# Moving a kernel's output transfers to another queue, its later states to a DMA transpose, more buffers for one small tile, and two smaller changes at its start

## The chip, the cores and the metric

One core of one Trainium2 chip. The metric is the device time of one execution in microseconds (us), lower is better; several executions are taken and their median is quoted. Beside it stands the **span**, the length of the one profiled execution from its first to its last instruction, which is about 2 us shorter than that execution's time. Executions of one kernel spread by up to some 1.5% here; one that is more than 1.5% above the fastest of its kernel is called slow, and only fast ones are compared. The experiments ran on several chips, and each took the kernel before along on its own chip, which is what the ratios are made of.

## The reference

Eight batches of attention between 512 tokens and 32 states in 8 heads of 64, then a feed-forward block with the maximum of three products, over all 8 × 544 rows.

```python
# x: (8, 8, 512, 64), state: (8, 8, 32, 64)
a  = softmax(scale * x @ state^T);   xread = a @ state
a2 = softmax(scale * state @ x^T);   sread = a2 @ x
y  = concat([xread, sread], axis=2)            # -> rows (batch, 512+32), 512 columns
h  = max(y @ w1, y @ w2, y @ w3)               # w: 512 x 768
out = h @ w_out                                # 768 x 512, float32
```

## The kernel before

A batch is prepared while the one before it goes through the feed-forward block. For a batch, x is loaded and cast by GpSimd's DMA queue (`load_x`), transposed by a DMA on SyncE's queue (`xT`), multiplied with the states (`scores`, which need xT), normalised by GpSimd (`a`), and a is transposed by DMA (`aT`). The second softmax gives `sr`, which a small DMA transpose puts into `ats`. `G` holds the states times the weights, so that `maxout` needs only aT and G.

```python
    def x_transpose_dma(b):
        new(xT, b, [128, H, 2, 128], "xT")
        nc.sync.dma_start_transpose(out=xT[b].rearrange("p h j t -> p (h j) t"), in_=x_sb[b][:, 0:XW])
    # ... cut ...
    def states_rest():
        st = data.tile([128, 16, 2, D], BF16, name="st")
        for c in range(2):
            nc.gpsimd.tensor_copy(out=st[:, :, c, :], in_=st_f)
        # ... cut: 16 TensorE transposes, copies by VectorE and ScalarE into bdr ...
    # ... cut ... end of sread(b):
        sr = work.tile([128, 2, D], BF16, tag="sr", name="sr")          # two buffers
        nc.vector.tensor_mul(out=sr, in0=p[:, :, 0, :], in1=rd.to_broadcast((128, 2, D)))
        late.append(lambda: nc.sync.dma_start_transpose(
            out=ats[:, b].rearrange("p s n -> p (s n)"), in_=sr.rearrange("p g d -> p (g d)")))
    # ... cut ... end of ffn_out(b, j): two transfers of 512 KB for a batch, at j = 1 and j = 3
        j0 = j if b == B - 1 and j >= 2 else j - 1
        if j == 1 or j == 3 or j0 == j:
            nc.sync.dma_start(
                out=out[b * SP:b * SP + S, :].rearrange("(p j) f -> p j f", j=J)[:, j0:j + 1, :],
                in_=o[:, j0:j + 1, :])
    # ... cut ... the loop: six slots for a batch, n = b + 1
            slots[0].append(lambda: scores(n, 0, 2))
            slots[0].append(lambda: softmax(n, 0, 2, nc.gpsimd.tensor_mul))
            slots[1].append(lambda: g_cols(n, (0, 1)))
            slots[2].append(lambda: a_transpose_dma(n))
            slots[3].append(lambda: sread(n))
            # ... cut ...
                slots[3].append(lambda: x_transpose_dma(n + 1))
            slots[4].append(late_transposes)
                slots[1].append(lambda: load_x(n + 2))
        for m in (1, 2, 4, 5):           # ffn_out of the batch before: j = 0, 1, 2, 3
            if pending:
                slots[m].append(lambda t=pending.pop(0): ffn_out(*t))
```

Slot 2 thus issues aT and then the first output of the batch before (j = 1, its half of 512 KB); slot 3 issues xT of the next batch but one.

The softmax here doesn't subtract the row's maximum and nothing guards it: scores larger than these inputs give would overflow.

Of the kernel before, what the change touches and what calls it, by code (L numbers as in the profile page):

```python
# [15 lines left out]
def kernel(  # L16
# [39 lines left out]
    E = 2  # L56
# [30 lines left out]
    def load_w(c):  # L87
        m0, m1 = chunks[c]
        for i, w in enumerate((moe_w1, moe_w2, moe_w3)):
            nc.gpsimd.dma_start(  # L90
                out=w_sb[c][:, :, i, :],
                in_=w.rearrange("(kk p) f -> p kk f", p=128)[:, :, m0 * 128:m1 * 128])

    def w_cols(m):
        c = [m0 <= m < m1 for m0, m1 in chunks].index(True)
        f = (m - chunks[c][0]) * 128
        return w_sb[c], slice(f, f + 128)

    load_w(0)
    bde = data.tile([128, E, H, 2, Ns], BF16, name="bde")  # L100
    nc.vector.memset(bde, 0.0)
# [4 lines left out]
    load_w(1)  # L106
    load_x(1)
    load_w(2)
    load_w(3)
    load_x(2)  # L110
    nc.gpsimd.dma_start(out=wout_sb, in_=moe_w_out.rearrange("(kk p) f -> p kk f", p=128))
# [6 lines left out]
    def keep_busy(n):  # L118
        p = pp.tile([128, 1024], F32, tag="two", name="idle")
        for _ in range(n):  # L120
            nc.tensor.matmul(p[:, 0:512], zero[:, 0:128], zero, start=True, stop=True)
# [4 lines left out]

    def states_early():
        st = data.tile([128, 2 * E, 2, D], BF16, name="ste")
        nc.vector.tensor_copy(out=st, in_=st_early_f.unsqueeze(2).to_broadcast((128, 2 * E, 2, D)))
        p = pp.tile([128, 2 * E, 128], BF16, tag="pw", bufs=4, name="pte")  # L130
        for t in range(2 * E):
            nc.tensor.transpose(p[:, t, :], st[:, t].rearrange("p c d -> p (c d)"), ident)
        for c, copy in enumerate((nc.vector.tensor_copy, nc.scalar.copy)):
            r = slice(64 * c, 64 * c + 64)
            copy(out=bde[r, :, :, c, :].rearrange("p b h n -> p (b h) n"),
                 in_=p[r].rearrange("p t (h n) -> p (t h) n", n=Ns))

    def states_rest():

        st = data.tile([128, 16, 2, D], BF16, name="st")  # L140
        for c in range(2):
            nc.gpsimd.tensor_copy(out=st[:, :, c, :], in_=st_f)  # L142
        for k in range(2):
            p = pp.tile([128, 8, 128], BF16, tag="pw", bufs=4, name="pt")
            for t in range(8):
                nc.tensor.transpose(p[:, t, :], st[:, 8 * k + t].rearrange("p c d -> p (c d)"), ident)
            for c, copy in enumerate((nc.vector.tensor_copy, nc.scalar.copy)):
                r = slice(64 * c, 64 * c + 64)
                dst = bdr[r, :, :, c, :].rearrange("p b h (q t) -> p (b h) q t", t=16)
                copy(out=dst[:, :, :, 8 * k:8 * k + 8],  # L150
                     in_=p[r, :, 16 * E:16 * B].rearrange("p t (k q) -> p k q t", q=2))


    xT, e, a, aT, G, ht, osb = {}, {}, {}, {}, {}, {}, {}
# [4 lines left out]
    def x_transpose(b, g, copy):  # L159

        if g == 0:
            new(xT, b, [128, H, 2, 128], "xT")
        p = pp.tile([128, HS, 2, 128], BF16, tag="pw", bufs=4, name="pxt")
        for s in range(HS):
            for jj in range(2):
                nc.tensor.transpose(  # L166
                    p[:, s, jj, :],
                    xv[b][:, 2 * s + g, 2 * jj:2 * jj + 2, :].rearrange("p j d -> p (j d)"), ident)
        copy(out=xT[b].rearrange("p (s g) j t -> p g s j t", g=2)[:, g], in_=p)
# [24 lines left out]
    def softmax(b, g0, g1, mul):  # L194
        n = g1 - g0
        if g0 == 0:
            new(a, b, [128, J, 2, HS, Ns], "a")
        den = work.tile([128, J, n, HS], F32, tag=f"den{n}", name="den")
        nc.vector.reduce_sum(out=den, in_=e[b][:, :, g0:g1], axis=AX.X)  # L199
        rden = work.tile([128, J, n, HS], F32, tag=f"rden{n}", name="rden")  # L200
        nc.vector.reciprocal(out=rden, in_=den)  # L201
        mul(  # L202
            out=a[b][:, :, g0:g1].rearrange("p j g s n -> p j (g s) n"),
            in0=e[b][:, :, g0:g1].rearrange("p j g s n -> p j (g s) n"),
            in1=rden.rearrange("p j g s -> p j (g s)").unsqueeze(3).to_broadcast((128, J, n * HS, Ns)))
# [17 lines left out]
    def sread(b):  # L223

        p = pp.tile([128, 2, 2, D], F32, tag="pw", bufs=4, name="psr")
        for j in range(J):
            for g in range(2):
                for s in range(HS):
                    xj = xv[b][:, 2 * s + g, j, :]
                    both = bass.AP(xj.tensor, xj.offset,  # L230
                                   (xj.ap[0], (XW - ((2 * s + g) * J + j) * D, 2), (1, D)))
                    nc.tensor.matmul(  # L232
                        p[32 * s:32 * s + 32, g], e[b][:, j, g, s, :], both,
                        start=(j == 0 and g == 0), stop=(j == J - 1), skip_group_check=True,
                        tile_position=(0, 32 * s))
        rd = work.tile([128, 2, 1], F32, tag="rd", name="rd")
        nc.vector.reciprocal(out=rd, in_=p[:, :, 1, 0:1])
        sr = work.tile([128, 2, D], BF16, tag="sr", name="sr")
        nc.vector.tensor_mul(out=sr, in0=p[:, :, 0, :], in1=rd.to_broadcast((128, 2, D)))  # L239
        late.append(lambda: nc.sync.dma_start_transpose(  # L240
            out=ats[:, b].rearrange("p s n -> p (s n)"), in_=sr.rearrange("p g d -> p (g d)")))


    def g_cols(b, ms):
        for m in ms:
            if m == 0:
                new(G, b, [128, 2, NM * 384], "G")
            w, f = w_cols(m)
            p = pp.tile([128, 2, 512], F32, tag="two", name="pg")
            for s in range(HS):  # L250
                for g in range(2):
                    nc.tensor.matmul(  # L252
                        p[32 * s:32 * s + 32, g, 0:384].rearrange("p (i f) -> p i f", i=3),
                        bd(b, 2 * s + g)[64 * g:64 * g + 64, g, :], w[64 * g:64 * g + 64, s, :, f],
                        start=True, stop=True, tile_position=(64 * g, 32 * s))
            nc.scalar.copy(out=G[b][:, :, m * 384:(m + 1) * 384], in_=p[:, :, 0:384])  # L256


    def maxout(b, m, n, lhs, rhs, nk):
# [14 lines left out]
    def x_maxout(b, m):  # L274
        maxout(b, m, 512,
               lambda i, k: G[b][:, k, m * 384 + i * 128:m * 384 + i * 128 + 128],
               lambda k: aT[b][:, :, k, :], 2)
# [6 lines left out]
    def ffn_out(b, j, split=False):  # L284
        if j == 0:
            osb[b] = work.tile([128, J, d_model], F32, tag="osb", name="osb")
        p = pp.tile([128, d_model], F32, tag="pw", bufs=4, name="po")
        for m in range(NM):
            nc.tensor.matmul(p, ht[b][:, m, j * 128:(j + 1) * 128], wout_sb[:, m, :],  # L289
                             start=(m == 0), stop=(m == NM - 1))  # L290
        o = osb[b]
        if split:
            nc.scalar.copy(out=o[:, j, 0:256], in_=p[:, 0:256])
            nc.vector.tensor_copy(out=o[:, j, 256:512], in_=p[:, 256:512])
        else:
            nc.scalar.copy(out=o[:, j, :], in_=p)  # L296
        if b == "s":
            for k in range(4 * j, 4 * j + 4):
                r0 = k * SP + S
                (nc.sync if k % 4 < 2 else nc.gpsimd).dma_start(  # L300
                    out=out[r0:r0 + Ns, :], in_=o[32 * (k % 4):32 * (k % 4) + 32, j, :])
            return
        j0 = j if b == B - 1 and j >= 2 else j - 1
        if j == 1 or j == 3 or j0 == j:
            nc.sync.dma_start(
                out=out[b * SP:b * SP + S, :].rearrange("(p j) f -> p j f", j=J)[:, j0:j + 1, :],
                in_=o[:, j0:j + 1, :])

# [3 lines left out]
            late.pop(0)()  # L312

    dve, act = nc.vector.tensor_copy, nc.scalar.copy
    keep_busy(5)
    states_early()
    dve(out=xv[0].rearrange("p (s g) j d -> p g s (j d)", g=2)[:, 0], in_=x0_f[0])
    act(out=xv[0].rearrange("p (s g) j d -> p g s (j d)", g=2)[:, 1], in_=x0_f[1])
    x_transpose(0, 0, dve)
    x_transpose(0, 1, dve)  # L320
    for g in range(2):
# [3 lines left out]
    a_transpose(0, 0, act)  # L325
    a_transpose(0, 1, dve)
    x_maxout(0, 0)
    g_cols(0, (1, 2))
    sread(0)
    x_transpose(1, 0, dve)  # L330
    x_transpose(1, 1, dve)
    x_maxout(0, 1)
    scores(1, 0, 2)
    softmax(1, 0, 2, nc.gpsimd.tensor_mul)
    x_maxout(0, 2)
    g_cols(0, (3,))
    g_cols(1, (0, 1))
    x_maxout(0, 3)
    sread(1)
    g_cols(0, (4, 5))  # L340
    states_rest()
    x_transpose_dma(2)
    x_maxout(0, 4)
    g_cols(1, (2, 3))
    a_transpose(1, 0, act)
    a_transpose(1, 1, dve)
    x_maxout(0, 5)
    g_cols(1, (4, 5))


    pending = [(0, j) for j in range(J)]
# [63 lines left out]
```

## Time and profile before

| | before |
|---|---|
| time | 182.09 us, median of 3 (180.52 to 182.64) |
| span | 179.5 us, mean granted TensorE clock 0.968 |
| scores matmuls of batches 2 to 7 start at | 36.47, 61.29, 79.86, 98.38, 115.73, 131.86 |
| periods between them | 24.8, 18.6, 18.5, 17.35, 16.1 |

The kernel has one spine: the scores matmuls of each batch. Nothing of a batch can go on before them, so their distance is the batch's period, and the time is *start of the first of the steady ones + five periods + a tail*. Here 36.47 + 95.39 + 47.64 = 179.5. (The prediction reads the last two starts as 115.89 and 132.02; the timeline's rows have 115.73 and 131.86, and nothing hangs on that.)

The two views to hold on to are the shares of the chain that ended last, and the list of DMA issues (transfer, queue that issued it, count, KB of each, median us from issue to landing). Before:

```profile
PE 55%; DMA 16%; DVE 13%; ACT 5%; SPq 4%; issue 3%; POOL 2%; DVEq 0%; ACTq 0%; POOLq 0%
...
out_dram<-osb SPq DMA_DIRECT2D x15, 512.0 KB, 3.0
...
xT<-x SPq DMA_TRANSPOSE x6, 9.5
```

The chain runs mostly through TensorE. The median output lands 3.0 us after it was issued and the median xT after 9.5 us, from the same queue. A median hides something here: the four outputs that are issued just ahead of an xT, with x's load still running, take 6.5 to 9.4 us.

### The profile page before, as it was taken

Reading aid. Unit: us, or ns where it says so; the run is one execution under the profiler, and the core shown is the slowest. Engines: PE = TensorE matmul, PEld = TensorE weight load, DVE = VectorE, ACT = ScalarE, POOL = GpSimd, SP = SyncE. Lnnn points to the kernel's source line nnn. Section 1 sums busy time; section 2 is a strip of 40 time slices with the busy share of each in tenths; the row PEclk is TensorE's granted clock in tenths of the full one; section 3 lists DMA queues with packets and bytes.
Section 4 is the critical chain, followed back from the end, with each engine's and each line's share of the span. In section 5 each row is a group of like instructions: output and inputs, shape, how many; then the busy total and the mean of one; then the engine's idle time right before and its main releaser. Section 6 shows DMA issues by size and latency. Waiting matters only on the chain.

```text
span 179.5 us, 3488 instructions
## 1 busy us (share of the span) xinstructions
PE 151.5 (84%) x1390; PEld 70.0 (39%) x1405; DVE 96.3 (54%) x167; ACT 96.4 (54%) x153; POOL 34.5 (19%) x39
## 2 busy tenths in 40 slices
PE   5467975899806999949995999999999999999991
PEld 1242633343301434423432344434344447566440
DVE  5384885675205386437653636486557638555200
ACT  3342675894501774828373646783785582344340
POOL 8774252006000050003200230040004000000040
PEclk9999999999975999999999699999999999999998
DMA  4999999902991209990795269617631502020354
GB/s 138 300 194 190 195 201 200 138 5 40 198 171 23 109 14 121 201 198 17 96 216 108 117 82 226 167 64 168 135 121 23 160 4 119 0 117 0 121 197 155
DMA packets 39008, 22.64 MB, mean 126 GB/s; under 512 B 24464, under 2 KB 36496, under 8 KB 38992
## 3 DMA queue, kind: packets, MB, share of 16 engines
q1 hardware_dynamic: 23936, 15.21, 36.7%
q0 software_dynamic: 14528, 7.08, 30.8%
q8 instruction: 11, 0.18, 0.4%
q10 hardware_dynamic: 528, 0.13, 0.3%
q14 instruction: 5, 0.04, 0.1%
HBM read 15.34 MB, written 8.91 MB: 135 GB/s over the span
## 4 chain that ended last, share of the span: by engine, by line
PE 55%; DMA 16%; DVE 13%; ACT 5%; SPq 4%; issue 3%; POOL 2%; DVEq 0%; ACTq 0%; POOLq 0%
PE pw L266 27%; PE po L289 19%; DMA xT<-x 12%; DVE den L199 4%; SPq L173 4%; ACT e L192 3%; PE pg L252 3%; DVE ht L272 3%; DMA stef<-in_state_dram 3%; DVE t L271 2%; PE ps L187 2%; PE pxt L166 2%; DMA ats<-sr 1%; PE psr L232 1%; POOL st L142 1%
## 5 line engine op out<-in xcount | busy, mean ns | idle before, releaser
L266 PE MATMUL pw<-aT,G 128*128 128x512 bf16 x288 | 74.9, 392 | 8.9 <-DVE sr L239 6.7
L271 DVE TENSOR_TENSOR t<-t,pw 128x512 bf16<-128x512 bf16 (+1 forms) x54 | 35.0, 649 | 41.7 <-ACT t L270 38.8
L289 PE MATMUL po<-wout,ht 128*128 128x512 bf16 x189 | 48.5, 383 | 1.0 <-issue 0.2
L266 PEld LDWEIGHTS <-G 128*128 128x128 bf16 x288 | 27.3, 100 | 42.6 <-issue 7.9
L270 ACT CAST t<-pw 128x512 bf16<-128x512 f32 (+1 forms) x54 | 30.6, 566 | 23.8 <-PE pw L266 22.3
L256 ACT CAST G<-pg 128x768 bf16<-128x768 f32 x48 | 36.0, 802 | 12.2 <-PE pg L252 11.9
L272 DVE TENSOR_TENSOR ht<-t,pw 128x512 bf16<-128x512 bf16 (+1 forms) x54 | 35.5, 657 | 5.6
L202 POOL TENSOR_TENSOR a<-e,rden 128x1024 bf16<-128x1024 bf16 x7 | 13.3, 1905 | 99.6 <-DVE rden L201 53.9
L296 ACT COPY osb<-po 128x512 f32<-128x512 f32 x33 | 19.3, 585 | 23.2 <-PE po L289 22.8
L289 PEld LDWEIGHTS <-ht 128*128 128x128 bf16 x204 | 18.6, 98 | 25.7 <-issue 7.0
L199 DVE TENSOR_REDUCE den<-e 128x32 f32<-128x1024 bf16 (+1 forms) x9 | 9.9, 1099 | 7.0 <-ACT e L192 7.0
L192 ACT ACTIVATE e<-ps 128x1024 bf16<-128x1024 f32 x7 | 7.2, 1023 | 9.3 <-PE ps L187 9.3
L252 PE MATMUL pg<-w,bdr 64*32 64x384 bf16 x288 | 10.0, 347 | 0.0
L90 POOL DMA_DIRECT2D w<-in_moe_w_dram x12 | 9.4, 799 | 2.4 <-DMA w<-in_moe_w_dram 2.3
L300 POOL DMA_DIRECT2D out_dram<-osb x4 | 2.1, 523 | 35.3 <-ACT osb L296 35.1
L266 PE MATMUL pw<-ats,w 128*128 128x256 bf16 x72 | 8.8, 273 | 0.0
L187 PEld LDWEIGHTS <-xT 128*128 128x128 bf16 x128 | 5.1, 102 | 7.2 <-DMA xT<-x 5.5
L266 PEld LDWEIGHTS <-w 128*128 128x128 bf16 x72 | 7.0, 98 | 2.1
L187 PE MATMUL ps<-bdr,xT 128*128 128x64 bf16 x96 | 3.8, 193 | 4.5 <-DMA xT<-x 4.5
L239 DVE TENSOR_TENSOR sr<-psr,rd 128x128 bf16<-128x128 f32 x8 | 2.3, 291 | 9.0 <-DMA ats<-sr 8.8
L79 POOL DMA_DIRECT2D x<-in_x_dram x7 | 6.4, 918 | 0.6 <-DMA w<-in_moe_w_dram 0.6
L252 PEld LDWEIGHTS <-bdr 64*32 64x32 bf16 x288 | 2.5, 90 | 8.4 <-issue 8.4
(46 smaller groups left out, 56.5 us busy)
## 6 DMA issues: line engine op xcount, KB each, us to landing
out_dram<-osb SPq DMA_DIRECT2D x15, 512.0 KB, 3.0
x<-in_x_dram POOLq DMA_DIRECT2D x7, 512.0 KB, 10.4
w<-in_moe_w_dram POOLq DMA_DIRECT2D x6, 256.0 KB, 9.4
x0f<-in_x_dram SPq DMA_DIRECT2D x2, 512.0 KB, 5.1
w<-in_moe_w_dram POOLq DMA_DIRECT2D x6, 128.0 KB, 8.3
wout<-in_moe_w_out_dram POOLq DMA_DIRECT2D x1, 768.0 KB, 13.1
stf<-in_state_dram SPq DMA_DIRECT2D x1, 512.0 KB, 6.6
out_dram<-osb SPq DMA_DIRECT2D x2, 256.0 KB, 2.2
```

The source lines that it names most:

```text
L187: nc.tensor.matmul(p[:, 2 * jj:2 * jj + 2, g - g0, s, :], xT[b][:, h, jj, :], bd(b, h).rearrange("p c n -> p (c n)"), start=(g == g0 and s ...
L192: nc.scalar.activation(out=e[b][:, :, g0:g1], in_=p, func=AF.Exp, scale=scale)
L199: nc.vector.reduce_sum(out=den, in_=e[b][:, :, g0:g1], axis=AX.X)
L202: mul(out=a[b][:, :, g0:g1].rearrange("p j g s n -> p j (g s) n"), in0=e[b][:, :, g0:g1].rearrange("p j g s n -> p j (g s) n"), in1=rden.r ...
L252: nc.tensor.matmul(p[32 * s:32 * s + 32, g, 0:384].rearrange("p (i f) -> p i f", i=3), bd(b, 2 * s + g)[64 * g:64 * g + 64, g, :], w[64 * ...
L256: nc.scalar.copy(out=G[b][:, :, m * 384:(m + 1) * 384], in_=p[:, :, 0:384])
L266: nc.tensor.matmul(p[:, 0:n], lhs(i, k), rhs(k), start=(k == 0), stop=(k == nk - 1))
L270: nc.scalar.copy(out=t0[:, 0:n], in_=pw[0][:, 0:n])
L271: nc.vector.tensor_max(t1[:, 0:n], t0[:, 0:n], pw[1][:, 0:n])
L272: nc.vector.tensor_max(ht[b][:, m, :], t1[:, 0:n], pw[2][:, 0:n])
L289: nc.tensor.matmul(p, ht[b][:, m, j * 128:(j + 1) * 128], wout_sb[:, m, :], start=(m == 0), stop=(m == NM - 1))
L296: nc.scalar.copy(out=o[:, j, :], in_=p)
```

## The change

Its intent: keep output transfers from standing between the transposes on SyncE's queue; take work off TensorE, VectorE and ScalarE at the start; have TensorE at full clock when data arrives; remove a wait for the two `sr` buffers. The diff, with the parts that only follow from it cut, as is the move of one early block of G ahead of another:

```diff
+    st = data.tile([128, 16, 2, D], BF16, name="st")
+    stT = data.tile([128, 16, 128], BF16, name="stT")
+    def states_rest_cast():            # called after load_w(2), ahead of load_w(3), load_x(2)
+        for c in range(2):
+            nc.gpsimd.tensor_copy(out=st[:, :, c, :], in_=st_f)
+        nc.sync.dma_start_transpose(out=stT, in_=st.rearrange("p t c d -> p (t c d)"))
 ...
-    def states_rest():                 # casts, 16 TensorE transposes, copies by VectorE, ScalarE
+    def states_rest_place():
         for c in range(2):
+            r = slice(64 * c, 64 * c + 64)
+            nc.gpsimd.tensor_copy(
+                out=bdr[r, :, :, c, :].rearrange("p b h (q t) -> p (b h) q t", t=16),
+                in_=stT[r, :, 16 * E:16 * B].rearrange("p t (k q) -> p k q t", q=2))
 ...
-        sr = work.tile([128, 2, D], BF16, tag="sr", name="sr")
+        sr = work.tile([128, 2, D], BF16, tag="sr", bufs=B, name="sr")
 ...
-            nc.sync.dma_start(
+            (nc.sync if b == B - 1 else nc.gpsimd).dma_start(
                 out=out[b * SP:b * SP + S, :]. ... [:, j0:j + 1, :], in_=o[:, j0:j + 1, :])
 ...
-    keep_busy(5)
+    keep_busy(12)
 ...                                    # early copies: ste by ScalarE, x of batch 0 by VectorE
-    g_cols(0, (1, 2))
+    g_cols(0, (1, 2), (act, dve))      # and three more of batch 1
```

## The prediction

> **What bounds the kernel now.** I read the page first (busy shares, the forty slices), then the chain of work that ended last in order of time, then TensorE's own waits, then the SyncE queue's timeline. The page's slices:
>
> ```profile
> PE   5467975899806999949995999999999999999991
> PEclk9999999999975999999999699999999999999998
> DMA  4999999902991209990795269617631502020354
> ```
>
> A slice is 179.5/40 = 4.49 us. TensorE is nearly full from slice 12 on, so the second two thirds are bound by matmuls. It is not full in slices 0 to 11, and slice 11 is empty; where it was empty the granted clock falls (slices 11, 12, 22). DMA is full from slice 1 to slice 7 (4.5 to 36 us) and again in bursts. TensorE's waits, from 40 to 170 us, are few and large:
>
> ```profile
> PE pw L266 <- DVE sr L239: 6.7, 1, 6.7
> PE ps L187 <- DMA xT<-x: 4.5, 2, 2.3
> PE pw L266 <- DVE ht L272: 1.0, 5, 0.2
> ```
>
> The chain shows how the 6.7 us comes about, and the shape of one of the two 2.3 us waits:
>
> ```profile
> 46.15 6.30 SPq L173
> 52.50 2.32 DMA ats<-sr
> 54.92 0.30 DVE sr L239
> 55.27 2.74 PE pw L266 x6
> ...
> 66.13 0.59 PE pw L266 x2
> 66.72 1.31 PE po L289 x6
> 68.06 0.59 ACT osb L296
> 68.67 0.43 SPq L305
> 69.19 10.63 DMA xT<-x
> 79.86 0.65 PE ps L187 x16
> ```
>
> First group: there are only two sr buffers. VectorE cannot write batch 2's sr until batch 0's sr has been transposed out, and that transpose stands in the SyncE queue behind the 512 KB transpose xT (its issue alone took 7.87 us). VectorE stops, PSUM is not emptied, TensorE stops, and the next six matmuls take 2.74 us where six otherwise take 1.3: it came back at half clock. Second group: xT of the next batch is issued only after an output transfer, which itself waited for ScalarE's osb. The transpose lands 10.63 us later and the scores matmuls wait for it. The SyncE queue's timeline:
>
> ```profile
> 66.83 1.26 SPq L218 DMA_TRANSPOSE aT<-a  x1
> 68.67 0.43 SPq L305 DMA_DIRECT2D out_dram<-osb  x1
> 69.19 7.27 SPq L173 DMA_TRANSPOSE xT<-x  x1
> ```
>
> So a batch's period is the distance between scores matmuls. In the timeline these start at 36.47, 61.29, 79.86, 98.38, 115.89 and 132.02: periods of 24.8, 18.6, 18.5, 17.5, 16.1. The last has no x load beside it and no wait; I take **16.1 us as the TensorE-bound period**.
>
> **What the Trainium skill says.** (1) "DMA: Bandwidth & Descriptors", section "Issuing engines are not separate DMA queues": transfers issued by any engine end on the same 16 DMA engines, and a second issuer saves only issue time. The trace agrees as to rate: from 10 to 33 us the bytes per second stay near 200 GB/s, whether the GpSimd queue runs alone or xT runs beside it. (2) The same page, "Queues, rings and completion order", says that an engine takes turns between queues, packet by packet. The trace hardly shows turns: xT of batch 2, issued at 26.57, moved no packet until about 30.6, while 200 to 350 packets per us went on the GpSimd queue. The measurement decides: a transpose issued into a backlog waits for much of it. (3) "TensorE: Matmul & The Clock Gate", "Part 1: The HAM clock gate": half clock by default, full clock after about 3.4 us of sustained work, measured in a free-running window. The trace agrees: the five warm-up matmuls start 0.43 us apart, end at 3.5 us and did not suffice; 128x512 matmuls still come 0.42 us apart at 16 us and 0.215 us apart after 19.5 us. (4) "SBUF — State Buffer" warns that some VectorE operations lock GpSimd out of writing its descriptors. The trace of before can't show this for outputs; its x loads in the loop issue in 0.94 us beside a busy VectorE, so I charge nothing for it.
>
> **The change part by part.**
> *Eight sr buffers.* The write-after-read wait goes, with it the 6.7 us and the cold restart (2.74 - 1.3 = 1.4 us, and 0.3 us on the next sixteen): 8.4 us on the path. The period 24.8 becomes at best 16.1, else whatever xT allows.
>
> *Outputs on the GpSimd queue.* Eleven or so 512 KB outputs leave the SyncE queue; aT is then followed directly by xT. At the chain above xT could issue at 66.83 + 1.26 = 68.1 in place of 69.19: 1.1 us earlier. It also no longer stands behind the output in its own ring. Packets per us show that xT's bulk ran only after that output had landed (issued 87.25, landed after 9.4, i.e. 96.6; 1,707 of xT's 2,048 packets moved from 96 to 98). What remains ahead of xT is x's load (active 88 to 93.5). Against that the output now stands in the loads' queue, behind which transposes seem to wait. GpSimd pays an issue of 0.5 to 0.9 us per output (rows of 523 and 918 ns) and is 19% busy; in its order every output precedes only work that comes later anyway. Estimate: xT 0.5 to 2 us earlier, periods 18.6 and 18.5 become about 17.2, 17.5 becomes 17.2.
>
> *Later states by DMA transpose.* Removed: sixteen transposes on TensorE (1.07 us), 1.81 us of VectorE, 1.66 us of ScalarE, and the wait for GpSimd's casts: in the chain from 26.26 to 31.6, of which some 4 us are on the path. Added: one transpose of 128x2048 bf16, the size of xT, in the time when DMA is full. Alone xT takes 3.4 us of issue and lands after 5.2. The DMA was busy until 35.57, when xT of batch 2 landed (26.57 + 9.0), only 0.7 us before the scores matmul that reads it. With 2.5 to 3.4 us more to move, it lands at 38 to 39. Then GpSimd places the states: 2 copies of 1536 elements per partition, at the 1.03 us per 1024 of its casts some 1.5 us each, 3.1 us in all; if the states' transpose waits for the load backlog (to 31 us) it lands at 34 to 35.5 and the placing ends at 37.5 to 39. Either way scores of batch 2 start at about **38.8**, not 36.47: 2.3 us **lost**.
>
> *Warm-up of 12 and shared copies.* 12 x 0.43 = 5.2 us from 1.19: TensorE is busy to 6.3 and should then run at full clock. The path from 6.02 to 17.73 holds about 6 us of TensorE at half clock, so 3 us less, and ste and x move off each other's engine for a little more. But batch 1's x lands at 17.15 (the GpSimd queue waits for it until then) and its transposes ran at 18.67: at most 1.5 us of it survive there, and TensorE, which I expect at batch 2's scores by about 32, then waits some 6 us for xT. Value at the end: nothing.
>
> **Sum.** Scores of batch 2 at 38.8; four periods of 17.2 with x loads (68.8), one of 16.1: the last scores matmul at 123.7 where it was 132.0. After it nothing changes but the outputs' queue: 179.5 - 132.0 = 47.5, so a span of 171.2. The profiled run's time exceeded its span by 1.9 (181.42 against 179.5) and the median is 0.7 above that run: 171.2 + 2.6 = 173.8. I state 174.3, as the wait at 32 to 38 may bring the half clock back.
>
> **Rivals.** (a) *Transposes starve behind the outputs too.* The GpSimd queue then carries x and two outputs per batch, and xT lands no earlier than before: periods stay at 18.5. For it: the silent 4 us after 26.57, and that all bytes still cross the same engines. Against: xT's bulk followed the output's landing, in its own ring. Result: 38.8 + 4 x 18.5 + 16.1 + 47.5 = 176.4, as a time 179. (b) *The start hides or costs more.* If GpSimd's strided placing takes 3 us a copy in place of 1.5, or the casts, now ahead of four loads, delay batch 2's x by their 2 us, the loop begins at 41 to 42: 2 to 3 us worse, 176 to 177. Conversely, if the DMA had slack for the states' transpose, it begins at 35: 170. (c) *TensorE-bound loop.* If xT is out of the way entirely, periods are 16.1: 4.4 us better, about 170. For it: only 2.3 us separate before from this.
>
> **Range and chances.** A and b together give just over 181, c with an early start 166. Neither end is likely; 8 in 10 from 169.5 to 179.5. Faster by 2% means under 178.4: only with rival a and some of b is it missed, 0.83. Within 2% 0.15; slower needs a new stall that I do not see, 0.02.
>
> **What would show each step.** Right: no wait for sr in TensorE's list, and periods of 16 to 17.5 between scores matmuls; xT issued directly behind aT; TensorE idle before batch 2's scores, released by xT or by the placed states (bdr), with scores at 37.5 to 40; transposes at 7 us at full clock (0.5 us for eight), yet batch 1's transposes not before 17.2. Wrong: periods of 18.5 with xT as releaser (rival a); scores of batch 2 before 36.5 (the DMA had slack); a wait of softmax on GpSimd behind an output; half clock before slice 4. The prediction fails as a whole if the start loses more than 6 us or the clock falls in several slices of the loop.

## The result, and the profile after

| | before | after |
|---|---|---|
| time, same chip | 182.37 us (180.52 to 183.33, 4 runs) | 198.81 us (197.65 to 201.02, 4 runs, the last slow) |
| ratio of fast runs | | 1.0917, 95% interval 1.0795 to 1.1039 |
| span, granted clock | 179.5 us, 0.968 | 196.9 us, 0.904 |
| scores of batch 2 start at | 36.47 | 40.01 |
| periods of batches 2→3 … 6→7 | 24.8, 18.6, 18.5, 17.35, 16.1 | 21.7, 22.9, 23.4, 23.5, 17.7 |
| xT landing after its issue, batches 3, 4, 5, 6 | 10.0, 10.6, 10.6, 8.0 | 14.5, 15.6, 16.1, 16.1 |

A ratio here is the mean time of one kernel's fast runs over that of the other's fast runs of the same rounds, so it is not quite the ratio of the medians quoted.

The kernel is 9% slower where 4% faster was expected. The span grew by 17.4 us: 3.5 up to the scores of batch 2, 13.8 in the five periods (109.2 against 95.4), 0.1 in the tail. The slices (tenths of busy time and of the clock in 40 equal parts of the span) after:

```profile
PE   7619959489964999289970999529999999999991
PEclk9975996969996699969996699957999999999999
DMA  5999999904999099913999069990952232011065
```

TensorE now has a hole in each of batches 3 to 6 (4, 2, 0 and 2 in slices 12, 16, 21 and 26), and at or behind each hole the clock falls to 6 or 5. Before, there were two such places. TensorE's waits from 40 to 170 us (line, what it waited for, us in all, times, longest) give one cause:

```profile
PE ps L189 <- DMA xT<-x: 24.2, 5, 6.1
```

The wait for sr, 6.7 us before, is gone. In its place the scores wait 24.2 us for xT, 4.5 before; 3.3 of the 24.2 are the wait before batch 2, the rest are the four holes. Chain shares and DMA issues, in the view shown of before:

```profile
DMA 50%; issue 21%; PE 14%; POOL 8%; SPq 2%; ACT 2%; DVE 2%; POOLq 0%; ACTq 0%; DVEq 0%
...
out_dram<-osb POOLq DMA_DIRECT2D x14, 512.0 KB, 6.2
...
xT<-x SPq DMA_TRANSPOSE x6, 15.0
```

Half of the chain is now DMA. One batch of it, in order of time (start, us, what):

```profile
113.99 1.25 SPq L220
...
115.28 0.03 SPq L175
...
115.34 16.12 DMA xT<-x
...
131.51 1.04 PE ps L189 x16
132.54 2.56 PE pw L268 x6
```

The first step of the prediction's reasoning came true: xT (line 175) is issued directly behind aT (line 220), 1.3 us after aT's start, where before it took 2.4 (66.83 to 69.19). But it lands 16.1 us later, not 10.6. The sixteen scores matmuls take 1.04 us in place of 0.63 and the next six 2.56 in place of 1.3, which is the cold restart. What else is in flight is seen by laying SyncE's queue (first two lines) beside GpSimd's (last three) for an earlier batch:

```profile
90.59 1.25 SPq L220 DMA_TRANSPOSE aT<-a  x1
91.93 7.45 SPq L175 DMA_TRANSPOSE xT<-x  x1
```

```profile
90.52 0.96 POOL L79 DMA_DIRECT2D x<-in_x_dram  x1
93.29 0.55 POOL L307 DMA_DIRECT2D out_dram<-osb  x1 [1.81 <-ACT osb L298]
```

x's load, aT, xT and the output are all issued within 3 us. Before, the output went ahead of xT in the same queue and landed first (at 96.61 for the xT that landed at 98.33); most of xT then moved with no output beside it. Now they run at the same time (this output lands at 107.61, its xT at 108.01). The DMA view of one microsecond of each (queue, packets, MB, share of 16 engines): before, from 97 to 98, and after, from 104 to 105. Queue q1 carries the transposes, q0 what GpSimd issued.

```profile
q1 hardware_dynamic: 970, 0.24, 108.4%
```

```profile
q1 hardware_dynamic: 206, 0.05, 72.5%
q0 software_dynamic: 25, 0.08, 34.7%
```

Before, xT moved 970 packets in this microsecond. After, it moved 206, beside 25 large packets of the output.

### The profile page after: what moved, and what is told of

Read it like the earlier page. It is cut to its first block, busy times and chain, and to the rows that moved or that the text cites. A ratio compares the mean times of both kernels' runs of the same rounds, so it can differ in the third digit from the quotient of the medians.

```text
span 196.9 us, 3460 instructions
## 1 busy us (share of the span) xinstructions
PE 158.2 (80%) x1381; PEld 72.0 (37%) x1396; DVE 99.2 (50%) x167; ACT 93.1 (47%) x149; POOL 47.8 (24%) x55
## 4 chain that ended last, share of the span: by engine, by line
DMA 50%; issue 21%; PE 14%; POOL 8%; SPq 2%; ACT 2%; DVE 2%; POOLq 0%; ACTq 0%; DVEq 0%
DMA xT<-x 36%; DMA w<-in_moe_w_dram 11%; PE pw L268 7%; POOL a L204 4%; PE po L291 4%; PE ps L189 3%; DMA out_dram<-osb 3%; SPq L220 2%; POOL w L90 1%; PE pg L254 1%; POOL st L105 1%; POOL out_dram L307 1%; DVE den L201 1%; ACT t L272 1%; ACT e L194 1%
## 5 line engine op out<-in xcount | busy, mean ns | idle before, releaser
L268 PE MATMUL pw<-aT,G 128*128 128x512 bf16 x288 | 79.3, 414 | 1.4 <-ACT G L258 0.8
L273 DVE TENSOR_TENSOR t<-t,pw 128x512 bf16<-128x512 bf16 (+1 forms) x54 | 35.1, 649 | 45.9 <-ACT t L272 40.4
L258 ACT CAST G<-pg 128x768 bf16<-128x768 f32 x44 | 33.3, 802 | 20.8 <-PE pg L254 20.8
L268 PEld LDWEIGHTS <-G 128*128 128x128 bf16 x288 | 28.7, 104 | 37.3 <-issue 10.0
L272 ACT CAST t<-pw 128x512 bf16<-128x512 f32 (+1 forms) x54 | 30.5, 566 | 16.4 <-PE pw L268 15.0
L298 ACT COPY osb<-po 128x512 f32<-128x512 f32 x33 | 19.3, 586 | 21.3 <-PE po L291 19.4
L291 PEld LDWEIGHTS <-ht 128*128 128x128 bf16 x204 | 18.6, 98 | 25.3 <-issue 6.2
L307 POOL DMA_DIRECT2D out_dram<-osb x14 | 7.7, 550 | 80.9 <-ACT osb L298 80.9
L189 PE MATMUL ps<-bdr,xT 128*128 128x64 bf16 x96 | 5.8, 233 | 24.2 <-DMA xT<-x 24.2
L194 ACT ACTIVATE e<-ps 128x1024 bf16<-128x1024 f32 x7 | 7.2, 1024 | 31.8 <-PE ps L189 31.8
L189 PEld LDWEIGHTS <-xT 128*128 128x128 bf16 x128 | 6.2, 118 | 27.8 <-DMA xT<-x 26.7
L131 PE MATMUL idle<-zero 128*128 128x512 bf16 x12 | 4.9, 595 | 1.2 <-DVE zero L70 1.2
## 6 DMA issues: line engine op xcount, KB each, us to landing
w<-in_moe_w_dram POOLq DMA_DIRECT2D x6, 256.0 KB, 10.9
wout<-in_moe_w_out_dram POOLq DMA_DIRECT2D x1, 768.0 KB, 17.2
```

Source lines behind the costliest of these rows:

```text
L189: nc.tensor.matmul(p[:, 2 * jj:2 * jj + 2, g - g0, s, :], xT[b][:, h, jj, :], bd(b, h).rearrange("p c n -> p (c n)"), start=(g == g0 and s ...
L258: copy(out=G[b][:, :, m * 384:(m + 1) * 384], in_=p[:, :, 0:384])
L268: nc.tensor.matmul(p[:, 0:n], lhs(i, k), rhs(k), start=(k == 0), stop=(k == nk - 1))
L272: nc.scalar.copy(out=t0[:, 0:n], in_=pw[0][:, 0:n])
L273: nc.vector.tensor_max(t1[:, 0:n], t0[:, 0:n], pw[1][:, 0:n])
L291: nc.tensor.matmul(p, ht[b][:, m, j * 128:(j + 1) * 128], wout_sb[:, m, :], start=(m == 0), stop=(m == NM - 1))
```

## The experiments

Two families of theory stood against each other. (The texts written before the runs call the queue of one issuing engine its ring.)

- **Overlap**: an output in flight together with the next batch's xT delays that xT, whichever queue it comes from. Within it, **M** (mixing is costly: the two together take longer than one after the other) and **F** (they only share, the sum of work is kept, but xT, which is waited for, gets the short end).
- **Rivals**: it is something in GpSimd's queue itself (its place in the issue order, the loads it shares the queue with); or it is the states' new transpose, the warm-up or the new order of the early work that disturbs the loop; or it is the size of the output's packets, which come from runs of 4 KB.

All results in one table. "Start" is where the scores of batch 2 begin in the profiled execution.

| kernel | time, median us | ratio of fast runs to before (95%) | span | start | periods 2→3 … 6→7 | xT landing, batches 3 to 6 |
|---|---|---|---|---|---|---|
| after | 198.81 | 1.092 (1.080 to 1.104) | 196.9 | 40.0 | 21.7 22.9 23.4 23.5 17.7 | 14.5 15.6 16.1 16.1 |
| `a_out_sync` | 178.07 | 0.973 (0.962 to 0.983) | 175.4 | 40.1 | 18.1 18.5 17.7 17.1 16.3 | 7.5 10.6 9.8 9.2 |
| `b_out_gp` | 199.28 | 1.093 (1.081 to 1.104) | 197.7 | 37.3 | 27.6 19.9 23.0 24.4 17.5 | 12.5 13.0 15.6 17.0 |
| `a_no_mid_out` | 175.13 | 0.960 (0.952 to 0.968) | 173.1 | 40.1 | 17.5 17.3 17.3 17.1 16.3 | 8.3 10.4 10.4 10.2 |
| `a_out_act` | 181.42 | 0.992 (0.982 to 1.002) | 179.5 | 39.7 | 21.4 19.3 17.6 16.9 16.2 | 14.2 12.4 10.6 10.0 |
| `b_sr8` | 175.68 | 0.965 (0.958 to 0.973) | 173.1 | 36.9 | 17.9 18.8 18.4 17.35 16.1 | 9.8 10.8 10.5 8.0 |
| `b_sr8_xt_first` | 170.53 | 0.935 (0.929 to 0.941) | 169.0 | 38.0 | 16.4 17.2 16.65 17.0 16.1 | 9.1 10.3 9.7 10.1 |
| `a_out_late` | 176.68 | 0.970 (0.963 to 0.976) | 174.9 | 40.1 | 17.35 17.4 17.8 17.2 16.3 | 8.7 10.4 10.9 10.3 |
| `a_out_1kb` | 194.43 | 1.064 (1.053 to 1.074) | 196.1 (slow) | 39.7 | 22.0 22.0 22.9 23.5 18.1 | 14.8 14.6 15.6 16.2 |
| `a_first_out_only` | 196.73 | not given | 195.6 (slow) | 40.4 | 21.1 21.35 23.5 24.1 17.7 | 13.9 14.4 16.4 16.7 |
| `a_second_out_only` | 175.83 | 0.963 (0.954 to 0.973) | 174.3 | 39.7 | 18.5 17.2 17.2 17.9 16.3 | 8.8 10.2 10.3 11.0 |
| `d_sync_xt_first` | 174.83 | 0.959 (0.950 to 0.969) | 172.8 | 39.9 | 17.6 17.1 17.2 17.0 16.3 | 8.9 10.2 10.2 10.1 |
| `c_sync_xt_first` | 168.04 | 0.921 (0.914 to 0.929) | 166.7 | 36.0 | 16.5 17.2 17.1 16.1 16.1 | 9.2 10.2 10.2 9.0 |

### Which part of the change does it

**`a_out_sync`**: the change with its outputs put back on SyncE's queue.

```diff
-            (nc.sync if b == B - 1 else nc.gpsimd).dma_start(
+            nc.sync.dma_start(
```

> The changed kernel with its outputs back on the SyncE queue, all else kept. Theory M (outputs in another ring run packet by packet against the transpose xT and both crawl): periods between scores matmuls fall from 22 to 23.5 back to 17 to 18.5, scores of batch 2 stay at about 40, the time is 173 to 179. Rival S (the other parts, the later states or the early changes, set the period): stays above 190.

Measured: 178.07 us, 2.7% faster than before (the interval reaches to 1.7%, so against a line of 2% it is unclear). The 20.7 us between the medians of it and of the changed kernel are the outputs' queue alone. xT lands after 7.5 to 10.6 us again.

**`b_out_gp`**: the kernel before with that one line moved the other way.

> The kernel before with only the outputs of batches 0 to 6 on the GpSimd queue. Theory M: periods of 22 to 24, time 200 to 208 (the sr wait may stay or be hidden behind xT). Rival S: 178 to 184.

Measured: 199.28 us, just under the range of 200 to 208, with periods of 19.9 to 27.6. One line alone makes the loss, without new states, warm-up or copies. This rules out the other parts as its cause. The wait for sr, which is left in this kernel, grew to 9.5 us, as sr's transpose waits behind a slower xT.

**`a_no_mid_out`**: the change without the outputs of batches 0 to 6. Its output is wrong, which doesn't matter for the time.

```diff
-            (nc.sync if b == B - 1 else nc.gpsimd).dma_start(
+            if b == B - 1: nc.sync.dma_start(
```

> The changed kernel without the outputs of batches 0 to 6 (a wrong result on purpose), which takes the suspected transfer away. Theory M: xT lands about 8 to 10 us after its issue, beside the x load alone, periods 16.1 to 17, time 168 to 175. If periods stay above 20, the x load is the partner that slows xT, not the output.

Measured: 175.13 us, periods of 17.1 to 17.5, xT landing after 8.3 to 10.4 us. So without any output the loop is where the prediction had put it (17.2), and x's load alone, which stays, lets xT land after 10.4. It also bounds what outputs on the best queue can still cost.

**`b_sr8`**: the kernel before with eight sr buffers and nothing else.

```diff
-        sr = work.tile([128, 2, D], BF16, tag="sr", name="sr")
+        sr = work.tile([128, 2, D], BF16, tag="sr", bufs=B, name="sr")
```

> The kernel before with eight sr buffers and nothing else. The prediction's own step: the 6.7 us wait and its cold restart go, period after batch 2 falls from 24.8 to about 18, time 174 to 176. Rival (xT of batch 3 lands only then and takes over the wait): 178 or more.

Measured: 175.68 us, span 173.1, which is 6.4 us less than before; the first period falls from 24.8 to 17.9. The prediction's own figure for this part was 8.4 with an xT that does not wait; here an xT wait of 1.4 us takes the place of some of it. This one word gains more than the whole of `a_out_sync` does (175.68 against 178.07 us): by these medians the change's other parts, without the outputs' move, lose some 2 us.

### Queue or overlap

**`a_out_act`**: the change, with the outputs on ScalarE's queue.

```diff
-            (nc.sync if b == B - 1 else nc.gpsimd).dma_start(
+            (nc.sync if b == B - 1 else nc.scalar).dma_start(
```

> The changed kernel with the outputs of batches 0 to 6 issued by ScalarE instead of GpSimd: another ring, [...]not behind the x loads. Theory M: any second ring beside the transposes does it, xT still takes 14 us or more, time 193 to 200. Rival G (it is GpSimd's queue itself: its descriptors, or the output standing behind the x load there): xT lands in 9 to 11 us, time 173 to 180.

Measured: 181.42 us (one more run was slow, 188.94). It lies between the two expectations and in neither, and the batches tell why: in batches 3 and 4, where the output was issued 2.1 and 1.7 us after xT, the two ran interleaved and xT landed after 14.2 and 12.4 us; in 5 and 6, where it was issued 0.15 us after xT, it was through before xT's bulk, and xT landed after 10.6 and 10.0. So a queue other than GpSimd's does the same harm when its packets mix with xT's.

**`a_out_late`**: outputs stay on GpSimd's queue, but go as one transfer of 1 MB at the end of a batch, after xT's time.

```diff
-        j0 = j if b == B - 1 and j >= 2 else j - 1
-        if j == 1 or j == 3 or j0 == j:
+        j0 = j if b == B - 1 and j >= 2 else j - 1 if b == B - 1 else 0
+        if (b == B - 1 and j >= 1) or j == 3:
```

> The changed kernel, outputs still on the GpSimd queue, but one of 1 MB per batch at the end of the batch, when xT should have landed. Theory M: what hurts is an output running while xT runs; now they hardly meet, xT lands after 9 to 11 us, periods 17 to 18.5, time 174 to 182. Rival G (GpSimd's queue is bad for outputs whenever they run): stays above 192.

Measured: 176.68 us, within 1% of the kernel with no such outputs at all. The timelines of GpSimd and SyncE of one batch:

```profile
80.29 0.95 POOL L79 DMA_DIRECT2D x<-in_x_dram  x1
...
90.76 0.56 POOL L307 DMA_DIRECT2D out_dram<-osb  x1 [9.51 <-ACT osb L298]
```

```profile
81.70 7.37 SPq L175 DMA_TRANSPOSE xT<-x  x1
```

The same queue, the same bytes (in one transfer in place of two), only 9.1 us after xT's issue in place of 1.4: no loss. The queue as such is acquitted.

**`a_first_out_only` and `a_second_out_only`**: of the change's two outputs for a batch, only the one at j = 1 (beside xT) or only the one at j = 3. Their outputs are wrong, which doesn't matter for the times.

```diff
-        if j == 1 or j == 3 or j0 == j:
+        if j == 1 or b == B - 1 and (j == 1 or j0 == j):      # second: j == 3 in the first place
```

> The changed kernel, of each batch's two outputs on the GpSimd queue only the first (issued about 1.5 us after xT) kept, the second dropped: a wrong result on purpose. If the second output, which joins while xT still runs, makes up what the transfers alone did not show, xT lands after 12 to 13.5 us here, periods 18.5 to 20.5, time 179 to 187. If computation beside the transfers makes it up, xT still takes 15 to 16 us, periods 22 to 23.5, time 194 to 199.

> The converse: only the second output of each batch kept (issued when TensorE has done the batch's last output matmuls), the first dropped: a wrong result on purpose. Theory M: by itself it comes when xT has nearly landed, xT lands after 10 to 11 us, periods 17 to 17.8, time 174 to 177, as with one late output of 1 MB. If any output on this queue costs 5 us, the time is above 185.

Measured: the first output alone costs most or all of it (197.40, 196.05, 190.37 and 198.65 us; no ratio is given, since three of the runs count as slow beside the 190.37, and its profile is of such a run; its xT lands after 13.9 to 16.7 us). Even the one fast run, 190.37, is 14.5 us above the second output alone, which costs nothing (175.83 us). So it is the one 512 KB output issued some 2 us after xT (1.8 to 2.5 here), not the bytes in the loop.

**`a_out_1kb`**: each output of the change in two halves of columns, so that the runs written are 1 KB long. It was meant to make the output's packets smaller.

> The changed kernel, each 512 KB output cut into two of 256 KB by columns, so that its runs are 1 KB instead of 4 KB. If turns between rings go by packets of the output's size, the transposes get a larger share and xT lands after 11 to 14 us instead of 15 to 16, time 185 to 195. If the cost of mixing comes per turn and not by size, xT stays at 15 to 17 and the time at 196 to 203.

```diff
-            (...).dma_start(out=out[...][:, j0:j + 1, :], in_=o[:, j0:j + 1, :])
+            for c in range(2):
+                (...).dma_start(out=out[...][:, j0:j + 1, 256 * c:256 * c + 256],
+                                in_=o[:, j0:j + 1, 256 * c:256 * c + 256])
```

Measured: 194.43 us, 2.2% under the changed kernel by the two medians, and the intervals against before (1.053 to 1.074, and 1.080 to 1.104) do not meet, so there is a small gain. But the profile, which fell in a slow run, shows xT after 14.6 to 16.2 us, as in the changed kernel. The time lies in the first expectation's range, the landing outside it. But this run does not test packet size, because the edit did not change it: a pair of these half outputs that leaves GpSimd's queue with nothing beside it (174 to 179 us) moves its 0.52 MB in 128 data packets, which is 4 KB each, as the whole outputs of the changed kernel do. So the third rival, the size of the packets, stays untested, and where the 4 us come from is not known.

### What the overlap costs by itself

**`dma_alone`**: no attention, no feed-forward; transfers of these shapes by fours, alone and together. Wrong, one execution.

```python
    for i in range(N): transpose(i)                              # xT's size, on SyncE
    settle()
    for i in range(N): store(nc.gpsimd, i)                       # 512 KB output
    settle()
    for i in range(N): transpose(i); store(nc.gpsimd, i)         # both
    # ... cut: the same with nc.scalar, in turn on nc.sync, and with x loads ...
```

> Transfers alone, a wrong result on purpose: eight stages, each begun when the one before has landed, four transfers of a kind in each: transposes of xT's size on SyncE's queue; 512 KB outputs on GpSimd's; both at once; both at once with the outputs on ScalarE's; both in turn on SyncE's queue; x loads on GpSimd's; x loads beside transposes; x loads beside outputs on SyncE's queue. Theory M: transposes alone and outputs alone take 8 to 11 us each (four times 2 to 2.7), in one ring in turn 16 to 21, side by side in two rings clearly more than that sum, 25 to 35, on GpSimd's and on ScalarE's queue alike. Rival F (the engines are only shared fairly, and xT is late because it gets half): side by side takes the sum, 16 to 21, in either case.

| stage, four transfers of a kind | us from the first issue to the last landing |
|---|---|
| transposes alone (about 0.21 MB per us when running) | 11.9 |
| outputs alone, GpSimd (0.40 MB per us) | 7.2 |
| both, outputs on GpSimd | 18.9 |
| both, outputs on ScalarE | 17.6 |
| in turn on SyncE's queue | 17.6 |
| x loads alone | 14.3 |
| x loads and transposes | 25.5 |
| x loads and outputs on SyncE's queue | 19.2 |

Measured: 11.9 + 7.2 = 19.1, and both at once took 18.9. Over a whole stage M's loss does not show, and F's sum holds. What does change is who waits: the first transpose landed after 4.4 us alone, after 9.0 beside GpSimd's outputs and after 8.7 beside ScalarE's. For a while the outputs went at full rate with 40 to 100 transpose packets per us against some 850.

The stage's sum does not settle M for the kernel, though, and a kept trace does. Inside the stage the two mixed in earnest only from 45 to 50 us, and there they moved 0.88 MB in 5 us, 0.18 MB per us, less than either alone; the time was made up when the outputs and then the transposes ran nearly by themselves. In the changed kernel they mix for much longer. From 99 to 107 us, nearly the stretch from the landing of x (99.5) to that of xT (108.0), its two queues moved (queue, packets, MB, share of 16 engines):

```profile
q1 hardware_dynamic: 1653, 0.42, 85.8%
q0 software_dynamic: 142, 0.51, 33.3%
```

That is 0.93 MB in 8 us. At the rates that each kind had alone here it would be 0.42/0.21 + 0.51/0.40, some 3.3 us (an estimate from these traces). And in `a_no_mid_out`, at the same place in the batch (88.8 to 92.1 us), the transposes moved their 0.39 MB in 3.4 us with pauses, where the changed kernel took 8.5 from x's landing to xT's (7.5 to 8.5 in batches 3 to 6). So in the kernel M holds: while the two mix, both are slowed, and xT's delay is mostly lost throughput and not only a worse place in the order. Why the rate falls, no run shows.

**`dma_replay`**: one batch's transfers in the loop's order and distance (x load, aT, xT, output), without computation, three times for each queue. Wrong, one execution.

> The transfers of one batch with no computation beside them, a wrong result on purpose: in each of twelve stages x's load on GpSimd's queue, aT and xT on SyncE's; three stages without an output, three with one 512 KB output on GpSimd's queue some 2 to 3 us later, three with it on ScalarE's, three with it on SyncE's ahead of xT. In the kernels xT lands 10.4 us after its issue without outputs, 16 with them on GpSimd's queue, 10 to 14 on ScalarE's, 10.6 on SyncE's. If the transfers alone do it (theory M, in the order in which they meet), the same figures come back within 1.5 us. If computation is part of it (rival C: GpSimd's descriptors held up by VectorE, or traffic of the engines), GpSimd's stages take no more than 12 us.

| output | xT landing after its issue, three times | mean | mean, counted from x's load |
|---|---|---|---|
| none | 8.7, 9.0, 9.7 | 9.1 | 10.2 |
| GpSimd | 13.0, 12.2, 12.3 | 12.5 | 13.6 |
| ScalarE | 11.1, 11.8, 11.0 | 11.3 | 12.4 |
| SyncE, ahead of xT | 10.2, 10.1, 10.1 (xT issued 0.9 later) | 10.1 | 12.1 |

Measured: beside an output from GpSimd xT lands 3.4 us later. In the kernel it is 5.5 (10.4 to about 16). The result lies between what the theories expected: the overlap delays xT without any computation around, but by less. Against an output ahead of xT on SyncE's queue, which is the move that the change makes, the replay shows less still: counted from the issue of x's load, 13.6 against 12.1, 1.5 us, where the kernel has 17.0 against 12.5 (means of batches 3 to 6, after and before), 4.5 us. **`dma_replay_busy`**, the last run, tests the obvious reason, that the engines' own traffic takes the rest: the same with TensorE, ScalarE and VectorE kept busy.

> The replay of one batch's transfers once more (a wrong result on purpose), three stages without an output and three with one on GpSimd's queue, now with TensorE, ScalarE and VectorE kept busy beside it by matmuls and by copies out of PSUM that depend on nothing in it. If computation beside the transfers makes up the missing 2 to 3 us (rival C), xT lands after 14.5 to 16.5 us with the output where the idle replay had 12.2 to 13.0, and after about 10.4 without it where it had 8.7 to 9.7. If computation is not part of it, the figures of the idle replay come back within 0.7 us and the remainder stays open.

Measured: 9.6 without (9.0, 10.0, 9.7), 13.0 with the output (14.2, 11.3, 13.6): some 3.4 us again, on means of three that spread widely. Computation of this kind does not bring the missing 2 us. What makes the mixing worse in the kernel stays open: the kernel has transfers about that the replay lacks, such as the transpose of sr behind xT, and whether these are it was not tried.

### A better version

**`b_sr8_xt_first`**: eight sr buffers, outputs on SyncE, and xT issued in slot 2 directly behind aT, ahead of the output in the same queue.

```diff
             slots[2].append(lambda: a_transpose_dma(n))
+            if n + 1 < B:
+                slots[2].append(lambda: x_transpose_dma(n + 1))
             slots[3].append(lambda: sread(n))
 ...
-            if n + 1 < B:
-                slots[3].append(lambda: x_transpose_dma(n + 1))
```

> As b_sr8, and xT is issued on the SyncE queue directly behind aT, ahead of the output, in the same ring. Theory M (only mixing of rings hurts; in one ring the transfers follow each other): xT lands 8 to 10.5 us after an issue 1 us earlier, periods 16.1 to 17.4, time 169 to 174. If it is xT's early issue that makes it slow, periods go to 20 and more.

Measured: 170.53 us, 6.5% faster than before. This is what the change meant to reach by the other queue: xT directly behind aT, and the output not in its way. The output simply follows: in the first batch of the loop xT lands at 54.15 and the output, issued at 52.12 in the same queue, at 55.29.

**`d_sync_xt_first`** is the whole change with outputs on SyncE and that order; **`c_sync_xt_first`** is the same with the later states transposed by TensorE, as before the change.

> All of the change but the outputs' queue, with xT issued directly behind aT and ahead of the output in SyncE's queue. Scores of batch 2 at about 40 as in the changed kernel, periods 16.3 to 17.2: time 172 to 175. If the early part of the change were a gain, it would be under 170.

> As the last, but the later states made as in the kernel before (transposes on TensorE, copies by VectorE and ScalarE); the longer warm-up and the shared copies stay. If the states' transpose in the full DMA is what delays batch 2 (prediction: 2.3 us), scores of batch 2 come at 35.5 to 37 and the time is 168 to 171. If warm-up and copies delay it, it stays at 172 to 175.

Measured: 174.83 and 168.04 us. The second is the best of all, 7.9% faster than before, and correct. SyncE's queue and TensorE's wait for xT in it:

```profile
75.25 1.25 SPq L218 DMA_TRANSPOSE aT<-a  x1
76.60 6.83 SPq L173 DMA_TRANSPOSE xT<-x  x1
83.52 0.53 SPq L305 DMA_DIRECT2D out_dram<-osb  x1
```

```profile
PE ps L187 <- DMA xT<-x: 1.9, 3, 0.9
```

The pair prices the states: batch 2 starts at 39.85 with the states' DMA transpose and at 36.01 without, 3.8 us, and the periods of the loop lose another 2.2 in sum (85.3 against 83.1), which was not traced further. And `c_sync_xt_first` against `b_sr8_xt_first`, which differ by the warm-up, the shared copies and the order of one early block, hints at what those are worth: ratios 0.921 against 0.935, some 2.5 us, with intervals that just touch. The start (36.0 against 38.0) does not settle it, as kernels with the same early code start batch 2 anywhere from 36.5 to 38.0 (before, `b_sr8`, `b_out_gp`, `b_sr8_xt_first`). By the same measure the price of the states' transpose is good to about a microsecond: 39.7 to 40.4 in all nine kernels with it, 36.0 to 38.0 in the five without.

## Why the prediction was wrong, step by step

**The step that failed** is "Estimate: xT 0.5 to 2 us earlier, periods 18.6 and 18.5 become about 17.2, 17.5 becomes 17.2", in the part on outputs on the GpSimd queue. Its first half, the issue, held: xT was issued some 1.0 us earlier after aT. The step went wrong in taking the landing to follow from the issue: in batches 3 to 6 xT landed 14.5 to 16.1 us after it, where before it had been 8.0 to 10.6. In place of 17.2 the four periods were 21.7, 22.9, 23.4 and 23.5, together 22.7 us more; start (+1.2), last period (+1.6) and tail (+0.2) make up the rest of 196.9 - 171.2 = 25.7. `b_out_gp` shows that this part does it alone, `a_out_sync` that without it the rest is 2.7% faster, `a_out_late` and the pair of half-outputs that the overlap in time does it and the queue does not.

The prediction had seen the evidence: "xT's bulk ran only after that output had landed". It read this as a cost of the shared queue. It was the protection: with the output ahead in one queue, xT's bulk met no output and moved 970 packets in a microsecond. And it wrote down rival (a), that transposes starve behind the outputs too, but sized it as "no earlier than before", periods of 18.5. Once the mechanism was named, the landing had no reason to stop there: the output no longer lay in front of xT, finished, but beside it. Nothing in the prediction's sum stands for two transfers that slow each other: in the kernel the pair moved 0.93 MB in 8 us where the rates alone give some 3.3. `dma_replay` gives 3.4 us for the delay, the kernel 5.5; that difference stays open.

**Half clock**: that TensorE restarts cold after a hole was known from the one such hole before. That it would come in every batch follows from the wait (an argument; no run separates the two), and the last sentence of the prediction names it as the sign of failure ("the clock falls in several slices of the loop").

**Eight sr buffers**: right in kind. The wait is gone; in `b_sr8` it is worth 6.4 us of span against 8.4, as xT takes over part of the wait.

**Later states**: the direction was right and the size off, 3.8 us (d against c) where 2.3 were charged. The mechanism is in the start of the changed kernel; SyncE's queue, GpSimd, TensorE:

```profile
12.69 5.38 SPq L106 DMA_TRANSPOSE stT<-st  x1
...
30.91 4.99 SPq L175 DMA_TRANSPOSE xT<-x  x1
```

```profile
27.29 5.66 POOL L151 COPY bdr<-stT 64x1536 bf16<-64x1536 bf16 x2
```

```profile
40.01 1.03 PE L189 MATMUL ps<-bdr,xT 128*128 128x64 bf16 x16 [3.27 <-DMA xT<-x]
```

The states' transpose was issued at 12.69 and landed after 13.7 us. It did not wait out the loads, as one branch of the prediction had it; from 17 to 25 us it took turns with them almost packet for packet (341 transpose packets beside 339 load packets from 18 to 19 us). So it delayed the loads: batch 2's x was issued at 14.80, only 0.25 later than before, but landed at 30.8 us, 4.3 later than before (26.5), and xT, which needs it, was issued at 30.91 and landed at 40.0. The placing by GpSimd took 2.8 us a copy, not 1.5 (the size in rival (b)), but it ended at 32.95 and was never waited for. The scores waited for xT, as the prediction's list of signs allows, but the route was x's load.

**Warm-up and shared copies**: the value of nothing fits (TensorE waited 3.3 us for xT before batch 2 in any case), though no run takes them out of the changed kernel. The way there was not as predicted. The first transposes did run at full clock (eight in 0.61 us, 1.03 before), but TensorE then waited 2.4 us for VectorE's `a`, its granted clock was 0.50 to 0.56 from 12 to 18 us, and the first six feed-forward matmuls took 3.02 us as before and began at 15.28, not earlier than 14.71. So the 3 us credited to TensorE's early path never came, and the prediction's sign "half clock before slice 4" did.

**GpSimd behind an output**: right. An output's issue took 0.53 to 0.60 us there and the softmax never waited for one.

**Readings**: besides the two starts named above, which make the period 17.35 and not 17.5, "eleven or so" outputs were 14, and xT of batch 2 landed 0.9 us before its scores, not 0.7. None of these carries the miss.

## What to carry to other kernels

Before moving a transfer to another queue to let a waited-for one start earlier, ask what the shared queue had kept apart: here the order in one queue also kept the two from running together, and together they were slower than one after the other. Put the transfer that is waited for first, in the same queue, and let the one that nobody waits for follow it. Read a delay as issue, wait and movement separately; here the issue got 1 us better and the landing 5.5 us worse. And check in the trace that an experiment changed what it was meant to change: `a_out_1kb` left the packets as they were.

## What the Trainium skill lacked or had wrong

- "DMA: Bandwidth & Descriptors", "Rules for kernel authors", says that a transpose next to ordinary DMAs needs nothing. Every complete kernel among the experiments gave right results. As to time it lacks the price: xT landed after 14.5 to 16.1 us beside a 512 KB output in place of 8.3 to 10.4, and after 12.5 in place of 9.1 with no computation about; and the two together moved 0.93 MB in 8 us.
- The same page's "Issuing engines are not separate DMA queues" is borne out by the sum over a stage of `dma_alone` (11.9 + 7.2 = 19.1 us, measured 18.9). It says that a second issuer saves issue time and no more; it lacks what the interleaving can cost, and the outputs' queue was worth 20.7 us here (178.07 against 198.81).
- The same page's "Queues, rings and completion order" has an engine take turns between queues by packet. The states' transpose did so with the loads (341 packets beside 339 in a microsecond). Beside outputs and in the loop it did not come out as equal turns: 206 transpose packets with 0.05 MB beside 25 output packets with 0.08 MB. No run shows why.
- "Advanced Engine Details and Errata", "X-Bar Transpose (TRN2)", calls transposes as fast as regular DMAs, at 350 to 400 GB/s. Measured alone, SBUF to SBUF, they moved about 0.21 MB per us and in their best microseconds 0.29, plain outputs 0.40.
- No page gives the time of a whole strided bf16 tensor copy on GpSimd (costs per element of code that one writes for its cores are all there is): 2.8 us for 1536 elements per partition, where its contiguous cast of 1024 took 1.03.
